# A kernel written out instruction by instruction, with a new order: two-block starts for the lone tiles, a weight piece loaded in two parts, three-block score runs from tile 8, one more store on GpSimd's queue

## The chip, the cores and the metric

The kernel runs on one core of a Trainium2 chip. The metric is the device time of one execution in microseconds (us). Three runs of the kernel before gave 213.09, 213.46 and 214.23 us, so the median is 213.46 us.

The engines are named as in the profile: PE is TensorE, with PEld for its weight loads; ACT is ScalarE, DVE is VectorE, POOL is GpSimd and SP is SyncE. Each works off its own instructions in order. Copies between device memory and on-chip memory are done by 16 DMA engines; an instruction on ACT, POOL or SP only issues them.

## The reference

Attention over 4 batches, 8 heads, 768 positions and 64 elements per head is followed by a two-layer network on the result. All inputs and the output are float32.

```
scores = scale * q @ k^T - slope[h] * distance       # each row sees 8 global positions and the last 96
a      = softmax(scores);   x = a @ v                 # x viewed as 3072 rows of 512
h = x @ w_in                                          # 512 -> 2048
out = (h - tanh(h)) @ w_out                           # 2048 -> 512
```

## The kernel before, in words

**Tiles.** The 3072 rows are 24 tiles of 128 rows. Tiles 0 to 3 are the first tiles of the four batches and see only themselves (one block of keys); tiles 4 to 23 see themselves (block 0) and the tile before in their batch (block 1). Because a row sees 96 positions back and 8 global ones, two blocks of 128 keys are enough: the 8 global keys and values are copied into the first rows of the back block (steps K and V).

**Steps of a tile u.** Each step has a name that the order list uses:

- `lq.u`, `lk.u`, `lv.u`: load q, k, v. The q and k of tiles 0 and 1 come as float32 over the queues of ACT and SP and are cast on chip (`cq`, `ck`); all else is cast on its way by POOL's queue.
- `T.u`: transpose k and q. For u below 7 PE does it (lines 309 to 322) and `Te.u.j` copies the result out of PSUM (a copy, lines 230 and 232); from tile 7 it is a DMA transpose on SP (line 334).
- `S.n`: one run of score matmuls (line 353), 8 per block. A run holds the blocks of one tile, or from tile THREES on three blocks of neighbouring tiles. `E.u.o` (ACT, line 360) is the exponential of a block, `M.u.o` (DVE, line 364) multiplies it by a mask that was made once (`bm`, PE line 276, and `em`, ACT line 281).
- `AV.u` (PE, line 379) is the product with v, `R.u` (DVE, lines 387 and 388) divides by the sums and writes x; `X.u` (PE, line 399) transposes x for tiles below 8 and `Xe.u` copies it out; from tile 8 on `Xe.u` is a DMA transpose on SP.
- `m1.g.f` (PE, line 421): first matmul for a group g of tiles and for some blocks f of 128 columns of w_in, accumulated in one PSUM bank. Groups 0 and 1 are the single tiles 0 and 1 (the lone tiles), groups 2 to 6 are pairs, groups 7 to 9 fours. A bank holds 512 columns, so a lone tile takes four blocks f at a time, a pair two and a four one. `th.g.f` (ACT, line 431) is the tanh, `g.g.f` (DVE, line 437) the difference; after it the bank is free.
- `m2.u.c.a` (PE, line 446): second matmul, four steps per tile; `ev.u` copies the bank out on ACT or DVE, `st.u` (line 455) stores it. The last tile, 23, is cut into columns 0 to 384 and 384 to 512.
- `in.j` and `out.j`: loads of w_in and w_out by POOL. The pieces of w_in end at the blocks listed in `in_end`. `zero:b` is a matmul on zeros into bank b (line 542) that computes nothing that is used.

**What sets the order.** Nothing is scheduled by a program at build time: the string ORDER (lines 17 to 66) lists every step once, and each engine gets its steps in the sequence of that list. The string HOMES (lines 67 to 105) says which buffer and which of the eight PSUM banks each result uses. A step waits for its inputs and for the last reader of its buffer or bank. POOL's list holds nearly all loads and all stores but the last ones, and a step there that waits holds up those behind it.

The lines that the change touches besides the two strings are 155 (THREES), 182 (in_end), 529 (blocks of an m1) and 539 (who stores).

Of the kernel before, what the change touches and what calls it, by code (L numbers as in the profile page):

```python
# [23 lines left out]
m1.2.2 g.1.4 th.2.6 T.4 g.2.6 th.2.2 lv.5 m1.2.0 Te.4.0/d Te.4.1/a lv.6 m1.1.8 g.2.2 th.2.0 g.2.0 m1.0.8 th.1.8 g.1.8  # L24
S.4 th.0.8 lq.6 m1.2.8 E.4.1 K.4 g.0.8 m1.1.12 th.2.8 M.4.1 T.5 E.4.0 g.2.8 m1.0.12 lk.6 Te.5.1/d Te.5.0/a m1.2.12
M.4.0 out.2 th.1.12 S.5 th.0.12 g.1.12 m2.1.0.0 th.2.12 K.5 g.0.12 E.5.0 m1.2.10 g.2.12 out.3 E.5.1 m2.0.0.0 M.5.0
lk.9 m2.0.0.1 th.2.10 M.5.1 lq.10 AV.4 g.2.10 lv.8 m2.2.0.0 V.4 R.4 AV.5 lk.7 m2.3.0.0 V.5 lq.8 R.5 m2.1.0.1 lk.10
m1.2.14 T.6 th.2.14 X.4 Te.6.1/d m2.2.0.1 Te.6.0/a lq.9 g.2.14 Xe.4/a m2.0.0.2 S.6 m2.2.0.2 E.6.0 K.6 lv.7 m2.1.0.2
E.6.1 M.6.0 X.5 m2.3.0.1 Xe.5/d M.6.1 m2.2.0.3 AV.6 T.7 ev.2.0/a m2.0.0.3 R.6 m2.3.0.2 T.8 ev.0.0/a V.6 m1.3.12 T.9
m1.3.0 th.3.12 T.10 m2.1.0.3 g.3.12 th.3.0 m1.3.8 g.3.0 ev.1.0/a S.7 st.1.0 th.3.8 lq.18 X.6 E.7.1 K.7 m2.3.0.3 g.3.8  # L30
lq.11 Xe.6/d m1.3.10 E.7.0 ev.3.0/d lv.12 m1.3.2 M.7.1 th.3.10 lq.14 m1.3.4 M.7.0 th.3.2 lv.10 g.3.10 S.8 th.3.4 g.3.2
m1.3.6 lq.12 E.8.1 g.3.4 m1.3.14 lv.9 th.3.6 M.8.1 AV.7 lk.13 E.8.0 g.3.6 m2.4.0.0 lk.11 R.7 th.3.14 m2.4.0.1 lk.12
V.7 S.9 M.8.0 lk.14 X.7 g.3.14 E.9.1 m2.4.0.2 st.0.0 K.9 Xe.7/d m2.4.0.3 E.9.0 lq.13 M.9.1 S.10 ev.4.0/d lv.11 AV.8
E.10.1 M.9.0 T.11 m1.4.8 K.10 R.8 E.10.0 m1.4.10 T.12 M.10.1 m2.5.0.0 th.4.8 M.10.0 Xe.8 th.4.10 AV.9 g.4.8 m1.4.2
T.14 V.9 m1.4.6 g.4.10 th.4.2 R.9 lq.23 T.13 AV.10 th.4.6 m1.4.0 g.4.2 lk.16 Xe.9 m2.5.0.1 g.4.6 th.4.0 R.10 m2.5.0.2
# [73 lines left out]
def kernel(  # L109
# [350 lines left out]
    def op(key, eng, fn):  # L460
        acts[".".join(map(str, key))] = (eng, fn)
# [128 lines left out]
```

## Time and profile before

| what | value |
|---|---|
| time of the profiled execution | 212.97 us |
| its span, first to last instruction | 211.1 us |
| the three timed runs | 213.09, 213.46, 214.23 us |
| PE busy | 203.6 us (96%) |
| DVE, ACT, POOL busy | 131.4, 118.8, 78.0 us |
| w_in pieces of 256 KB, 512 KB: median from issue to landing | 6.1 us, 10.7 us |
| stores by POOL: median from issue to landing | 3.2 us |

The profile is one execution. It lists the busy time of each engine, a picture of the span in 40 slices, the DMA queues, the chain of work that ended last (followed back from the last instruction), and groups of instructions by source line with their mean time and what ended the idle time before them. The trace behind it answers finer questions: busy time in a stretch of time, or the instructions of one engine in order. The time of the execution is 1.87 us longer than its span; that part lies around the first and last instruction.

### The profile page before, as it was taken

To read this page: it belongs to the slowest core of one execution; us is meant where nothing else is said; L and a number is where in the kernel's file an instruction comes from. 1 tells how busy PE (TensorE), PEld (TensorE's weight loads), DVE (VectorE), ACT (ScalarE), POOL (GpSimd) and SP (SyncE) were. 2 spreads that over 40 slices of the span, in tenths; PEclk is the share of its full clock that TensorE was granted. 3 is DMA by queue.
4 is the path that set the end of the run, shared out by engine and by line. 5 is a ranking of instruction groups with operands and counts; after the bars stand their busy time and mean duration, and the time that the engine had idled before them with its cause. 6 is when DMAs were issued, how large, how long until landed. Compare 5 with 4: busy or idle time off the path is not lost.

```text
span 211.1 us, 4634 instructions
## 1 busy us (share of the span) xinstructions
PE 203.6 (96%) x1854; PEld 122.4 (58%) x1879; DVE 131.4 (62%) x269; ACT 118.8 (56%) x175; POOL 78.0 (37%) x103
## 2 busy tenths in 40 slices
PE   8988999999999999999999999999999999999993
PEld 2558886557758765876665444555554444444442
DVE  7686787444898784789565779758875355412100
ACT  3995694245865385667645777268363364315322
POOL 8985546611992339259042360032000010003040
PEclk9999999999999999999999999999999999999999
DMA  6999999999999999999999979319311010003035
GB/s 154 208 191 195 198 192 163 197 156 197 158 153 170 170 156 177 146 166 172 215 132 145 152 121 182 66 59 101 76 28 26 0 50 0 3 0 149 0 135 213
DMA packets 100884, 27.29 MB, mean 129 GB/s; under 512 B 91840, under 2 KB 99264, under 8 KB 100864
## 3 DMA queue, kind: packets, MB, share of 16 engines
q0 software_dynamic: 72544, 18.62, 83.5%
q1 hardware_dynamic: 27776, 7.87, 23.5%
q10 hardware_dynamic: 544, 0.52, 0.9%
q8 instruction: 14, 0.23, 0.4%
q14 instruction: 6, 0.05, 0.1%
HBM read 27.26 MB, written 6.29 MB: 159 GB/s over the span
## 4 chain that ended last, share of the span: by engine, by line
PE 89%; DMA 4%; POOL 4%; issue 1%; ACT 0%; POOLq 0%
PE ps L446 39%; PE ps L421 39%; PE ps L353 5%; PE ps L379 5%; DMA w_in_bf<-in_moe_w_in_dram 4%; POOL vb L298 2%; POOL kq L295 1%; POOL w_in_bf L301 1%; PE ps L399 1%; PE ps L313 0%; PE ps L322 0%; POOL rel L236 0%; ACT ot L230 0%; POOLq L236 0%; POOLq L571 0%
## 5 line engine op out<-in xcount | busy, mean ns | idle before, releaser
L421 PE MATMUL ps<-xT,w_in_bf 128*128 128x256 bf16 (+2 forms) x635 | 90.9, 293 | 0.8 <-DMA w_in_bf<-in_moe_w_in_dram 0.6
L446 PE MATMUL ps<-w_out_bf,g 128*128 128x512 bf16 (+2 forms) x381 | 88.2, 370 | 1.4 <-issue 0.6
L437 DVE TENSOR_TENSOR g<-ps,th 128x512 bf16<-128x512 f32 x96 | 65.3, 687 | 37.8 <-ACT th L431 36.5
L431 ACT ACTIVATE th<-ps 128x512 f32<-128x512 f32 x96 | 57.2, 599 | 51.4 <-PE ps L421 48.3
L421 PEld LDWEIGHTS <-w_in_bf 128*128 128x128 bf16 x640 | 56.4, 98 | 29.0 <-DMA w_in_bf<-in_moe_w_in_dram 0.7
L446 PEld LDWEIGHTS <-g 128*128 128x128 bf16 x400 | 36.9, 98 | 38.1
L360 ACT ACTIVATE pr<-ps 128x1024 bf16<-128x1024 f32 x44 | 43.0, 1024 | 11.9 <-PE ps L353 11.9
L455 POOL DMA_DIRECT2D out_dram<-ot x21 | 12.1, 581 | 87.5 <-ACT ot L230 70.0
L364 DVE TENSOR_TENSOR pr<-pr,mk 128x1024 bf16<-128x1024 bf16 x44 | 29.3, 686 | 6.5 <-ACT pr L360 6.0
L298 POOL DMA_DIRECT2D kq<-in_q_dram x19 | 17.0, 902 | 22.0 <-DMA qk<-kq 17.6
L298 POOL DMA_DIRECT2D vb<-in_v_dram x24 | 21.7, 909 | 5.8 <-DMA w_in_bf<-in_moe_w_in_dram 4.0
L230 ACT COPY ot<-ps 128x512 f32<-128x512 f32 (+2 forms) x19 | 10.7, 563 | 21.9 <-PE ps L446 18.9
L298 POOL DMA_DIRECT2D kq<-in_k_dram x19 | 17.2, 919 | 8.5 <-DMA qk<-kq 6.5
L388 DVE TENSOR_TENSOR x<-ps,rden 128x512 bf16<-128x512 f32 x24 | 16.6, 691 | 0.8
L379 PEld LDWEIGHTS <-pr 128*128 128x128 bf16 x352 | 13.5, 97 | 4.2 <-DVE pr L364 0.6
L379 PE MATMUL ps<-vb,pr 128*128 128x65 bf16 x352 | 14.5, 193 | 0.2 <-DVE pr L364 0.2
L353 PEld LDWEIGHTS <-qk 64*128 64x128 bf16 x352 | 9.9, 94 | 6.1 <-issue 4.7
L353 PE MATMUL ps<-qk 64*128 64x128 bf16 x192 | 9.5, 218 | 0.1
L387 DVE RECIPROCAL rden<-ps 128x8 f32<-128x8 f32 x24 | 4.8, 200 | 4.8 <-PE ps L379 4.8
L353 PE MATMUL ps<-qk,qk 64*128 64x128 bf16 x160 | 7.8, 217 | 0.0
L542 PE MATMUL ps<-zero 128*128 128x512 bf16 x17 | 6.3, 489 | 1.0 <-DVE vb L272 1.0
L232 DVE COPY qk<-qk 128x32 bf16<-128x32 bf16 x16 | 3.3, 251 | 5.1 <-PE ps L353 5.1
(43 smaller groups left out, 60.6 us busy)
## 6 DMA issues: line engine op xcount, KB each, us to landing
out_dram<-ot POOLq DMA_DIRECT2D x21, 256.0 KB, 3.2
vb<-in_v_dram POOLq DMA_DIRECT2D x24, 128.0 KB, 5.6
kq<-in_k_dram POOLq DMA_DIRECT2D x22, 128.0 KB, 5.3
kq<-in_q_dram POOLq DMA_DIRECT2D x22, 128.0 KB, 5.4
w_out_bf<-in_moe_w_out_dram POOLq DMA_DIRECT2D x4, 512.0 KB, 11.5
w_in_bf<-in_moe_w_in_dram POOLq DMA_DIRECT2D x3, 512.0 KB, 10.7
f<-in_q_dram ACTq DMA_DIRECT2D x2, 256.0 KB, 4.3
f<-in_k_dram SPq DMA_DIRECT2D x2, 256.0 KB, 4.8
```

The source lines that it names most:

```text
L230: nc.scalar.copy(out=out, in_=in_)
L298: eng(e).dma_start(out=dst, in_=rows_of(src, u).rearrange("h p d -> p h d"))
L353: nc.tensor.matmul(bank(("s", u, o), hh)[:, p * P : (p + 1) * P], buf(("qk", back[u] if o else u))[r, 1, p, :], buf(("qk", u))[r, 0, p, :] ...
L360: nc.scalar.activation(d, banks(("s", u, o), 0, 1), AF.Exp, bias=0.0, scale=scale)
L364: nc.vector.tensor_tensor(out=t, in0=t, in1=mk[:, mask_of(u, o)], op=ALU.mult)
L379: nc.tensor.matmul(t[:, h // (H // 2), h % (H // 2), :], buf(("p", u, o))[:, slot(h), :], buf(("v", back[u] if o else u))[:, h, 0 : Dh + 1 ...
L388: nc.vector.tensor_tensor(out=buf(("x", u)).rearrange("q (a h) d -> q a h d", a=2), in0=t[:, :, :, 0:Dh], in1=rden.to_broadcast([P, 2, H / ...
L421: nc.tensor.matmul(t[:, (f - f0) * n : (f - f0 + 1) * n], w_in_bf[j][:, c, fo : fo + P], x[:, c, 0:n], start=(c == 0), stop=(c == CD - 1),)
L431: nc.scalar.activation(h_view(buf(("th", g, f0)), g, m), h_view(bank(("h", g, f0)), g, m), AF.Tanh, bias=0.0, scale=1.0)
L437: nc.vector.tensor_tensor(out=buf(("g", g))[:, f0 : f0 + m, 0:n], in0=h_view(bank(("h", g, f0)), g, m), in1=h_view(buf(("th", g, f0)), g, ...
L446: nc.tensor.matmul(bank(part)[:, 0 : c1 - c0], buf(("g", g))[:, f, t * P : (t + 1) * P], w_out_bf[f // FJ][:, f % FJ, c0:c1], start=(f == ...
L455: eng(e).dma_start(out=out[turn_of[u] * P : (turn_of[u] + 1) * P, c0:c1], in_=buf(("ot", u))[:, c0:c1])
```

## The change

Four lines of code change, and both strings are new:

- THREES goes from 11 to 8: tiles 8, 9 and 10, which had three runs of two blocks, now have two runs of three, so there are 19 runs of scores in place of 20, with later numbers one lower.
- `in_end` gets one more end: the 512 KB piece of w_in with blocks 4 to 7 is now two pieces of 256 KB, and there are six loads of w_in.
- The first four blocks of a lone tile are now two steps of two blocks, each with its own tanh and difference over 256 columns in place of one over 512.
- The store of tile 22 moves from SP's queue to POOL's.
- ORDER lists the steps in a new sequence on every engine, with 14 zero matmuls in place of 17; HOMES assigns buffers and banks anew. Some copies change engine with it. Counted by the two lists, ACT has seven steps more (a cast of k, a copy of a transposed tile, two copies of a transposed x, one copy-out of a result, two tanhs) and DVE three fewer.

```diff
 ORDER = """
-lq.1 lk.1 zero rel ones.0 zero:7 dist lk.3 lq.0 lk.0 zero:7 zero:7 slopes table lq.3 zero:7 zero:7 lk.2 turn first
-zero:7 ident bm.0 lq.2 ones.1 lv.0 bm.2 em.0 cq.1/d lv.1 zero:7 ck.1/d em.2 zero:7 T.1 lv.2 cq.0/a zero:7 ck.0/d in.0
-zero:7 Te.1.1/d Te.1.0/a zero:3 T.0 in.1 S.1 Te.0.1/d Te.0.0/a lv.3 T.3 E.1.0 S.0 Te.3.0/d zero:7 in.2 E.0.0 T.2 M.1.0
-lk.4 zero:6 zero:6 Te.2.1/d Te.2.0/a zero:6 lq.4 M.0.0 Te.3.1/a S.2 lk.5 E.2.0 AV.0 AV.1 R.0 S.3 in.3 E.3.0 R.1 X.0
-zero:1 lq.5 zero:3 Xe.0/a M.2.0 X.1 bm.1 Xe.1/a M.3.0 AV.2 in.4 em.1 m1.1.0 R.2 out.0 AV.3 th.1.0 X.2 R.3 m1.0.0
-Xe.2/a g.1.0 X.3 th.0.0 lv.4 m1.0.4 Xe.3/d g.0.0 m1.2.4 out.1 th.0.4 lq.7 m1.1.4 g.0.4 th.2.4 lk.8 g.2.4 m1.2.6 th.1.4
...
+lq.1 lk.1 zero rel ones.0 zero:7 slopes lk.2 lq.0 lk.0 zero:7 zero:7 table lq.2 dist zero:7 zero:7 lq.3 turn bm.1
+first lk.3 ident bm.0 ones.1 em.1 lv.1 cq.1/d zero:7 ck.1/a lv.0 zero:7 em.0 T.1 in.0 cq.0/a zero:7 ck.0/d lv.2 zero:7
+Te.1.0/d Te.1.1/a zero:3 T.0 lv.3 S.1 Te.0.1/d Te.0.0/a zero:6 zero:6 E.1.0 in.1 S.0 T.2 in.3 E.0.0 M.1.0 T.3 in.2
+Te.2.0/d zero:1 Te.2.1/a AV.1 M.0.0 Te.3.0/a lq.4 S.2 Te.3.1/a R.1 AV.0 lk.4 E.2.0 S.3 R.0 E.3.0 in.4 M.2.0 X.0 zero:3
+Xe.0/a in.5 M.3.0 AV.2 X.1 bm.2 R.2 Xe.1/a lk.5 AV.3 m1.0.0 em.2 R.3 m1.1.0 X.2 th.0.0 lq.5 X.3 th.1.0 Xe.2/d m1.1.2
+Xe.3/a g.1.0 m1.0.2 g.0.0 th.1.2 out.0 m1.2.2 th.0.2 g.1.2 g.0.2 m1.2.6 th.2.2 lv.4 g.2.2 m1.2.4 th.2.6 lk.6 g.2.6
...
-    THREES = 11
+    THREES = 8
...
-    in_end = [2, 4, 8, 12, 16]
+    in_end = [2, 4, 6, 8, 12, 16]
...
-        for f in range(0, CF, m):
+        for f, m in ([(0, 2), (2, 2)] if m == 4 else []) + [(f, m) for f in range(4 if m == 4 else 0, CF, m)]:
...
-            op(("st", u, c0), POOL if u < NU - 3 else SP, lambda e, u=u, c0=c0, c1=c1: store(e, u, c0, c1))
+            op(("st", u, c0), POOL if u < NU - 3 or u == NU - 2 else SP, lambda e, u=u, c0=c0, c1=c1: store(e, u, c0, c1))
```

Three more places of the new order, taken from it by engine. On SP the DMA transposes begin T.9 T.7 T.8 T.10 (before: T.7 T.8 T.9 T.10). On POOL the load of v for tile 8 stands behind st.1 and thirteen other loads: st.1.0 lv.7 lv.11 lq.14 lv.12 lv.16 lq.13 lq.11 lv.10 lv.9 lk.12 lq.12 lk.11 lk.14 lv.8. And the last stores on POOL are st.14 st.19 st.6 st.12 st.17 st.16 st.22 st.20 st.18, with the results of tiles 19, 17 and 20 in turn in output buffer 0, and those of tiles 22 and 21 in buffer 1.

More of the change, by code (lines that the diff above doesn't have):

```diff
@@ new lines @@
+th.2.10 m1.2.8 g.2.10 E.4.0 out.1 K.4 m1.1.8 E.4.1 M.4.0 out.2 m1.0.12 th.1.8 lq.9 M.4.1 th.2.8 T.5 g.1.8 th.0.12
+m1.1.12 Te.5.0/d Te.5.1/a g.0.12 m1.0.8 th.1.12 g.2.8 lv.5 m1.2.12 g.1.12 th.0.8 lq.10 g.0.8 m2.2.0.0 th.2.12 out.3
+g.2.12 m1.2.14 lk.7 m2.3.0.0 th.2.14 lk.9 g.2.14 T.6 AV.4 Te.6.1/d Te.6.0/a m2.0.0.0 V.4 R.4 m2.1.0.0 lq.7 S.5
+m2.2.0.1 E.5.1 K.5 m2.1.0.1 lk.8 E.5.0 M.5.1 m2.0.0.1 lq.8 M.5.0 S.6 lk.10 m2.1.0.2 E.6.1 K.6 m2.0.0.2 E.6.0 M.6.1
+AV.5 M.6.0 m2.3.0.1 R.5 X.4 m2.3.0.2 Xe.4/a V.5 X.5 m2.2.0.2 T.9 Xe.5/a AV.6 m1.3.0 T.7 R.6 m2.0.0.3 V.6 th.3.0 T.8
@@ new lines @@
+Xe.14 m2.9.0.2 V.14 g.6.6 AV.15 m2.9.0.3 R.15 m2.11.0.0 V.15 ev.9.0/a Xe.15 st.9.0 m2.11.0.1 lk.22 S.14 lv.20
+m2.10.0.0 E.17.0 K.17 st.7.0 m2.10.0.1 E.17.1 lv.18 M.17.0 m2.11.0.2 E.18.0 lq.22 M.17.1 AV.16 lv.22 m2.11.0.3 M.18.0
+R.16 lq.21 m1.7.7 ev.11.0/a V.16 Xe.16 lk.21 m2.10.0.2 th.7.7 st.8.0 g.7.7 m2.10.0.3 S.15 ev.10.0/a T.22 st.10.0
+m1.7.0 E.18.1 K.19 lq.20 m1.7.4 th.7.0 M.18.1 lk.23 E.19.0 m1.7.15 g.7.0 th.7.4 m1.7.13 M.19.0 th.7.15 g.7.4 T.21
+m1.7.10 th.7.13 g.7.15 m1.7.2 g.7.13 th.7.10 g.7.10 m1.7.1 th.7.2 g.7.2 AV.17 th.7.1 m1.7.3 V.17 E.19.1 g.7.1 T.20
@@ new lines @@
+m1.7.11 R.17 th.7.3 m1.7.6 g.7.3 T.23 th.7.11 M.19.1 m1.7.5 th.7.6 g.7.11 Xe.17 m1.7.12 g.7.6 th.7.5 g.7.5 AV.19
+th.7.12 m1.7.9 V.19 g.7.12 AV.18 R.19 th.7.9 m1.7.8 g.7.9 Xe.19 m1.7.14 th.7.8 R.18 m2.13.0.0 th.7.14 g.7.8 Xe.18
+g.7.14 m2.13.0.1 S.16 m2.13.0.2 E.20.1 K.20 K.21 m2.13.0.3 E.21.0 M.20.1 m2.12.0.0 ev.13.0/d E.20.0 M.21.0 m2.12.0.1
+M.20.0 S.17 m2.15.0.0 E.22.0 K.22 m2.15.0.1 E.21.1 M.22.0 AV.20 M.21.1 m2.15.0.2 E.22.1 R.20 m2.15.0.3 V.20 Xe.20
+M.22.1 S.18 ev.15.0/a AV.21 st.15.0 E.23.1 m1.8.1 R.21 st.13.0 E.23.0 st.11.0 m2.12.0.2 M.23.1 Xe.21 th.8.1 V.21
@@ new lines @@
+m1.8.4 M.23.0 g.8.1 AV.22 th.8.4 m1.8.9 V.22 R.22 m2.14.0.0 th.8.9 g.8.4 Xe.22 AV.23 g.8.9 m1.8.0 R.23 m1.8.15 th.8.0
+Xe.23 g.8.0 m1.8.8 th.8.15 g.8.15 m2.14.0.1 th.8.8 g.8.8 m1.8.3 m1.8.12 th.8.3 g.8.3 m1.8.5 th.8.12 g.8.12 m1.9.5
+th.8.5 g.8.5 m2.12.0.3 th.9.5 g.9.5 m1.9.9 ev.12.0/a m1.9.3 th.9.9 g.9.9 m1.9.1 th.9.3 g.9.3 m1.8.2 th.9.1 g.9.1
+m2.14.0.2 th.8.2 g.8.2 m1.8.7 m1.9.4 th.8.7 g.8.7 m1.8.14 th.9.4 g.9.4 m1.9.2 th.8.14 g.8.14 m1.8.6 th.9.2 g.9.2
+m1.9.6 th.8.6 g.8.6 m1.9.11 th.9.6 g.9.6 m1.9.14 th.9.11 g.9.11 m1.9.0 th.9.14 g.9.14 m2.18.0.0 th.9.0 g.9.0 m2.14.0.3
@@ new lines @@
+m2.16.0.0 ev.14.0/a st.14.0 m2.17.0.0 m2.22.0.0 m1.9.8 m2.16.0.1 th.9.8 g.9.8 m1.9.7 m1.9.15 th.9.7 g.9.7 m1.9.12
+th.9.15 g.9.15 m1.8.10 th.9.12 g.9.12 m1.8.11 th.8.10 g.8.10 m1.9.10 th.8.11 g.8.11 m2.22.0.1 th.9.10 g.9.10 m2.21.0.0
+m1.9.13 m2.18.0.1 th.9.13 g.9.13 m2.20.0.0 m2.20.0.1 m2.17.0.1 m2.19.0.0 m2.22.0.2 m1.8.13 m2.19.0.1 th.8.13 g.8.13
+m2.19.0.2 m2.17.0.2 m2.16.0.2 m2.16.0.3 m2.19.0.3 ev.16.0/a m2.18.0.2 ev.19.0/a st.19.0 m2.17.0.3 st.6.0 m2.21.0.1
+st.12.0 m2.22.0.3 ev.17.0/a m2.18.0.3 st.17.0 ev.22.0/a m2.20.0.2 st.16.0 st.22.0 ev.18.0/a m2.20.0.3 m2.21.0.2
@@ new lines @@
+kq.12:0 v.12:9 kq.13:1 v.13:5 kq.14:2 v.14:7 kq.15:3 v.15:6 kq.16:0 v.16:10 kq.17:1 v.17:4 kq.18:1 v.18:5 kq.19:3
+v.19:8 kq.20:2 v.20:0 kq.21:1 v.21:1 kq.22:0 v.22:9 kq.23:4 v.23:11 tr.0.0:5 tr.0.1:7 qk.0:1 s.0.0:2,3 p.0.0:1
+av.0:4,5 x.0:1 xt.0:0 xT.0:0 tr.1.0:6 tr.1.1:4 qk.1:0 s.1.0:0,1 p.1.0:0 av.1:0,1 x.1:0 xt.1:1 xT.1:1 tr.2.0:4 tr.2.1:5
+qk.2:2 s.2.0:2,3 p.2.0:2 av.2:2,3 x.2:2 xt.2:2 xT.2:2 tr.3.0:6 tr.3.1:7 qk.3:3 s.3.0:6,7 p.3.0:3 av.3:6,7 x.3:1 xt.3:3
+tr.4.0:3 tr.4.1:6 qk.4:4 s.4.0:0,1 s.4.1:6,7 p.4.0:4 p.4.1:0 av.4:4,5 x.4:0 xt.4:4 xT.3:3 tr.5.0:5 tr.5.1:0 qk.5:5
@@ new lines @@
+s.5.0:0,1 s.5.1:4,5 p.5.0:2 p.5.1:1 av.5:0,1 x.5:2 xt.5:5 tr.6.0:0 tr.6.1:6 qk.6:6 s.6.0:4,5 s.6.1:0,1 p.6.0:0 p.6.1:3
+av.6:0,1 x.6:1 xt.6:3 xT.4:1 qk.7:8 s.7.0:0,1 s.7.1:4,5 p.7.0:4 p.7.1:1 av.7:4,5 x.7:0 xt.7:3 qk.8:9 p.8.0:0 p.8.1:2
+av.8:6,7 x.8:0 xT.5:0 qk.9:7 s.8.0:0,1 s.8.1:4,5 s.9.0:6,7 p.9.0:3 p.9.1:1 av.9:6,7 x.9:2 qk.10:10 s.9.1:0,1
+s.10.0:4,5 s.10.1:6,7 p.10.0:1 p.10.1:4 av.10:2,3 x.10:1 xT.6:2 qk.11:5 p.11.0:3 p.11.1:0 av.11:4,5 x.11:2 qk.12:4
+s.11.0:6,7 s.11.1:4,5 s.12.0:2,3 p.12.0:2 p.12.1:4 av.12:2,3 x.12:0 xT.7:3 qk.13:1 s.12.1:2,3 s.13.0:4,5 s.13.1:0,1
@@ new lines @@
+s.22.0:4,5 s.22.1:0,1 p.22.0:0 p.22.1:2 av.22:4,5 x.22:1 qk.23:6 s.23.0:6,7 s.23.1:0,1 p.23.0:1 p.23.1:4 av.23:6,7
+x.23:2 h.0.0:0 th.0.0:0 g.0:1 h.0.2:5 th.0.2:3 h.0.4:2 th.0.4:1 h.0.8:2 th.0.8:3 h.0.12:4 th.0.12:0 h.1.0:1 th.1.0:1
+g.1:0 h.1.2:4 th.1.2:2 h.1.4:7 th.1.4:3 h.1.8:2 th.1.8:3 h.1.12:1 th.1.12:2 h.2.0:4 th.2.0:0 g.2:2 h.2.2:1 th.2.2:1
+h.2.4:6 th.2.4:2 h.2.6:0 th.2.6:0 h.2.8:3 th.2.8:1 h.2.10:5 th.2.10:2 h.2.12:0 th.2.12:0 h.2.14:1 th.2.14:1 h.3.0:4
+th.3.0:2 g.3:1 h.3.2:2 th.3.2:0 h.3.4:6 th.3.4:1 h.3.6:3 th.3.6:3 h.3.8:3 th.3.8:0 h.3.10:7 th.3.10:2 h.3.12:3
@@ new lines @@
+th.3.12:1 h.3.14:7 th.3.14:3 h.4.0:3 th.4.0:2 g.4:0 h.4.2:3 th.4.2:1 h.4.4:5 th.4.4:3 h.4.6:0 th.4.6:3 h.4.8:4
+th.4.8:2 h.4.10:0 th.4.10:0 h.4.12:0 th.4.12:1 h.4.14:2 th.4.14:0 h.5.0:5 th.5.0:1 g.5:2 h.5.2:0 th.5.2:1 h.5.4:1
+th.5.4:2 h.5.6:4 th.5.6:0 h.5.8:7 th.5.8:2 h.5.10:3 th.5.10:1 h.5.12:7 th.5.12:3 h.5.14:1 th.5.14:2 h.6.0:2 th.6.0:0
+g.6:1 h.6.2:7 th.6.2:2 h.6.4:6 th.6.4:3 h.6.6:6 th.6.6:1 h.6.8:0 th.6.8:3 h.6.10:6 th.6.10:0 h.6.12:5 th.6.12:0
+h.6.14:4 th.6.14:3 h.7.0:6 th.7.0:3 g.7:0 h.7.1:2 th.7.1:1 h.7.2:7 th.7.2:0 h.7.3:3 th.7.3:2 h.7.4:7 th.7.4:0 h.7.5:2
@@ L105 @@
+o.23.384:1
 """
```

113 lines of the change are left out of this document (34 added, 79 removed).

## The prediction

> **What bounds the kernel now.** I read the busy times first, then the busy time by stretch, then the chain that ended last, then PE's own rows at the start. The busy times:
>
> ```profile
> PE 203.6 (96%) x1854; PEld 122.4 (58%) x1879; DVE 131.4 (62%) x269; ACT 118.8 (56%) x175; POOL 78.0 (37%) x103
> ```
>
> PE is the bound, and no other engine is near it. By stretch (span and columns: stretch, its length, PE, PEld, DVE, ACT, POOL busy, granted clock, DMA share, GB/s):
>
> ```profile
> 0.00:18.43 18.43, 15.95 (x182) 8.94 (x184) 13.88 (x51) 13.37 (x18) 14.70 (x23) 1.00 1.34 186
> 18.43:60.00 41.57, 41.20 (x476) 30.41 (x482) 27.71 (x52) 25.89 (x39) 23.39 (x28) 1.00 1.74 180
> 60.00:120.00 60.00, 59.20 (x638) 40.22 (x646) 43.79 (x88) 36.68 (x51) 28.83 (x36) 1.00 1.63 164
> 120.00:165.00 45.00, 44.62 (x352) 22.68 (x358) 32.92 (x62) 25.92 (x39) 6.69 (x9) 1.00 0.57 80
> 165.00:207.84 42.84, 42.64 (x212) 20.13 (x212) 13.14 (x19) 16.72 (x30) 4.35 (x8) 1.00 0.16 58
> ```
>
> From 18.43 to 207.84 us PE idles 0.37 + 0.80 + 0.38 + 0.20 = 1.75 us of 189.4. Reordering has nothing to win there; it can only lose. What can shrink is the work in it, and the time before 18.43. The chain says what ends that time:
>
> ```profile
> 8.53 0.82 POOL vb L298
> 9.35 9.03 DMA w_in_bf<-in_moe_w_in_dram
> 18.38 0.05 issue
> 18.43 4.58 PE ps L421 x56
> ```
>
> The reader is to see that PE's dense part begins when the 512 KB piece of w_in (blocks 4 to 7, issued at 9.35) lands. PE's rows (start, length) just before it:
>
> ```profile
> 15.07 1.05 PE L421 MATMUL ps<-xT,w_in_bf 128*128 128x128 bf16 x16
> 15.96 0.41 PE L379 MATMUL ps<-vb,pr 128*128 128x65 bf16 x8
> 16.20 0.39 PE L399 MATMUL ps<-ident,x 128*128 128x128 bf16 x4
> 16.43 1.06 PE L421 MATMUL ps<-xT,w_in_bf 128*128 128x128 bf16 x16
> 17.46 0.40 PE L399 MATMUL ps<-ident,x 128*128 128x128 bf16 x4
> 18.43 4.58 PE L421 MATMUL ps<-xT,w_in_bf 128*128 128x128 bf16 x56 [0.57 <-DMA w_in_bf<-in_moe_w_in_dram]
> ```
>
> So at 18.43 PE has done T, S, AV and X of tiles 0 to 3, the three mask products, and m1 of both lone tiles for blocks 0 to 3. The question is when the new order has done the same list.
>
> **The start, step by step.** (1) Nothing moves up to S.1. T.0 waits for the cast of tile 0's k, which waits for a load that lands at 7.00 in both orders (DVE's cast there idles 1.48 us for it); S.1 stays at 8.08, E.1 and E.0 stay at 8.62 to 10.57. The cast of tile 1's k goes to ACT, between two mask exponentials: the first mask product ends at 4.0 (five warm-ups at 0.43 from 0.99, then two matmuls), the exponential starts 0.2 later, and 4.2 + 1.02 + 0.62 = 5.8, when T.1's weights were loaded before too (5.81), so nothing. (2) ACT now has three copies out of T.2 and T.3 in place of two, 0.55 each (row "1.10, x2"): E.2 starts at 10.45 + 3 x 0.55 = 12.1 (before 11.55), E.3 runs from 13.05 to 14.0 (before 12.74 to 13.76). This costs. (3) DVE gets that back. It does M.1, one copy and M.0 at a pace of 0.60 (starts 9.77, 10.37, 10.97), free at 11.6; before it then idled to 12.17 for an AV. Now AV.1 stands right behind M.1, so R.1 and R.0 (0.85 each) run from 11.6 to 13.35, M.2 to 14.0, M.3 after E.3 to 14.7; before M.3 ended at 15.14. (4) PE: X.0 at 13.45 (before 13.16), AV.2 at 14.05, X.1 and bm.2 (0.23 and 0.43), AV.3 at 15.05 (before 15.96). From there PE is dense: AV.3 0.3, m1.0.0 and m1.1.0 0.44 each (half of the 0.87 that 16 such matmuls take), X.2 and X.3 0.24 each, m1.1.2 and m1.0.2 0.44 each: 15.05 + 0.3 + 4 x 0.44 + 0.48 = 17.6. (5) m1.2.2 also needs the copy-out of X.3 on ACT. Before it stand em.2 (to 16.35) and two tanhs of 256 columns. No row shows that size: 128 columns take 0.265 (copy) and 512 take 0.60; I take 0.37, nearer the small end as in the 0.478 for 384. So Xe.3 runs from 17.05 to 17.6, and the list is done at 17.65: **0.78 us earlier**, by 0.57 of idle that goes and 0.2 of tighter packing.
>
> (6) Loads. The first 256 KB pieces take a median of 6.1 us from issue; the second, issued at 7.76, landed near 14.1, and 128 KB of v and 512 KB of w_in later it was 18.38: 6.7 ns per KB. In the new order blocks 2 and 3 lie behind one more v (15.0; needed 16.7), blocks 6 and 7 256 KB further (16.7; needed by m1.2.6 at 18.5), blocks 4 and 5 at the old end (18.4; needed by m1.2.4 at 19.4). What hides the split load is thus one step of m1 (m1.2.2) put ahead. If the piece were 1 us late, 0.1 would show. Two loads in place of one also cost POOL 0.78 us of issue, hidden since its loads then queue behind others for 9 us.
>
> Bounds of the start: a loss of 0.2 if the extra ACT copy (0.55) is not made good, and a gain of 1.1 if E.2's delay of 0.3 on M.3 does not count. I take 0.8.
>
> **Runs of three.** A run of 16 is followed by a hole or longer first matmuls:
>
> ```profile
> 41.95 0.55 PE ps L353 x16
> 42.50 0.16 issue
> ...
> 73.53 0.78 PE ps L353 x24
> ```
>
> Three runs of 16 become two of 24: 3 x 0.55 - 2 x 0.78 = 0.09, and one change-over less (0.10 to 0.16): **0.2 us**, bounds 0.1 and 0.3. The longer runs hold six banks of eight; after the second one, S.9, 2.8 us of other PE work precede AV.9, and the exponential and mask product that AV.9 waits for need 1.02 + 0.69 and some 0.3 of hand-overs, so that is covered by 0.8.
>
> **The rest at nothing.** ACT gets seven steps, some 3.5 us, against 92 us idle; DVE loses three. Three warm-up matmuls fewer leave holes that were filled with nothing. The end (last matmul at 207.84, span 211.10: 3.26) keeps its form: copy-out and store of the last 128 columns by SP. With tile 22's store on POOL, buffer 1 passes from 22 to 21 through POOL: ev.19, its store (2.8 to landing in the last rows), ev.17, ev.22, three stores of 0.55 of issue, 2.8 to landing, ev.21. Counted back from the last matmul, ev.19 ends 10.5 us before the end, ev.21 about 2.2 before it, and the last matmuls, which take its bank, start 0.9 before it: 1.3 us of room.
>
> **Sum.** 212.97 (profiled time) - 0.8 - 0.2 = 212.0. That execution is 0.49 under the median of 213.46; by that median it is 212.46. I predict **212.4**, nearer the median since timed runs carry no profiler. A measurement of this kernel can tell about 0.5% (1.07 us) from no change, so the border to faster is 212.39: the forecast lies on it.
>
> **The rivals.**
>
> *A, the start's gain is hidden (12%).* Xe.3, the m1.2.2 bank (freed by the difference for m1.1.0, at about 17.4) or a piece of w_in comes at 18.4 after all. For it: ACT carries E.2, E.3, two x copies, em.2, two tanhs and Xe.3 in one line. Against: each has 0.1 to 1 us to spare above. Time 212.4 + 0.8 = 213.2.
>
> *B, the array's pace falls back (10%), slower than before.* The row of granted clock says 1.00 throughout, but the first six warm-up matmuls stand 0.43 apart and three at 6.57 stand 0.215 apart: PE begins at half pace for 5 us of steady work. Before, PE was busy 0.71, 0.70 and 0.83 of each microsecond from 11 to 14 and kept the pace. In the new order, with fillers taken out, 10.75 to 13.45 holds only AV.0, S.2 and S.3: about 1.0 of 2.7. If that is under the point at which the pace falls, work from 14.05 on runs at half pace for 5 us and 2.2 us are lost: 212.4 + 2.2 = 214.6. Against: no single hole is above 1 us. The Trainium skill (TensorE: Matmul & The Clock Gate, Part 1: The HAM clock gate) states that the clock halves after an idle window of about 3.4 us; by that rule no hole here is long enough and B would not come.
>
> *C, a new wait in the dense part (8%).* First candidate is S.7 at about 51: SP sends T.9 before T.7, which costs 1.3 to 1.8 of issue, T.7 then leaves near 46.5 and lands 3.1 to 4.4 later, at 49.6 to 50.9. Second is AV.8 at 69: its v stands behind st.1 (about 50.3) and 13 loads of 0.9, issued at 62.6, landing 3.4 to 5.5 later. Third are banks: near the end a bank often returns after two m1 steps (1.73), and matmul to tanh to difference takes 1.52 (183.43 row group: difference ends at 185.81). Each could cost 0.3 to 1: 212.7 to 213.4.
>
> *D, more than the sum (8%).* Start 1.1 and runs 0.3, by the profiled time: 211.6.
>
> **How the numbers follow.** Forecast 62%, by itself 211.7 to 213.1; 37 points of it under 212.39. Faster: 37 + 8 (D) = 45%. Same: 25 + 12 (A) + 6 of C = 43%. Slower: 10 (B) + 2 of C = 12%. The range of 211.4 to 214.0 holds all but B and a few points at the ends.
>
> **What would show it.** Right: the dense part begins near 17.6 with no wait for w_in, the stretch from there to the last matmul is about 189.2 long, idle under 2 us in it, and the tail after it 3.3. Wrong: a wait for w_in or for Xe.3 before m1.2.2 (A); matmuls of 512 columns 0.43 apart after 14 us (B); PE waiting at S.7, AV.8 or in the last 45 us (C).

## The result, and the profile after

The kernel after takes 212.05 us (median of eight runs, 211.35 to 212.53); the kernel before, run beside it, takes 213.3 us (eight runs, 212.88 to 214.23). The ratio is 0.993, 95% interval 0.9911 to 0.9949: faster by 0.7%, and the interval lies just beyond the 0.5% that the forecast took as the least that can be told from no change. The forecast was 212.4. The profiled execution of after took 212.06 us with a span of 210.23; that of before 212.97 and 211.07 (the page rounds them to 210.2 and 211.1; the trace has the two decimals).

The busy times of after, and then its busy time by stretch (columns as before: stretch, its length, PE, PEld, DVE, ACT, POOL busy with counts, granted clock, DMA share, GB/s):

```profile
PE 202.4 (96%) x1851; PEld 122.3 (58%) x1876; DVE 130.0 (62%) x266; ACT 121.7 (58%) x182; POOL 79.2 (38%) x105
```

```profile
0.00:18.43 18.43, 14.82 (x181) 8.78 (x183) 12.49 (x49) 13.88 (x21) 15.29 (x24) 1.00 1.35 182
18.43:60.00 41.57, 41.30 (x481) 30.33 (x485) 27.51 (x52) 26.90 (x43) 22.96 (x28) 1.00 1.70 176
60.00:120.00 60.00, 59.42 (x635) 40.51 (x643) 43.52 (x85) 36.96 (x52) 32.54 (x41) 1.00 1.68 164
120.00:165.00 45.00, 44.62 (x352) 22.71 (x358) 34.21 (x64) 28.39 (x43) 3.57 (x6) 1.00 0.54 86
165.00:206.90 41.90, 41.74 (x204) 19.62 (x205) 12.30 (x18) 15.19 (x26) 4.82 (x9) 1.00 0.17 62
```

PE is the bound as before, idle for 0.27 + 0.58 + 0.38 + 0.16 = 1.39 us between 18.43 and 206.9 (1.75 before). The chain that ended last begins otherwise than before:

```profile
1.54 6.23 DMA f<-in_k_dram
7.77 0.02 issue
7.79 0.44 DVE kq L233
...
16.02 0.89 PE ps L422 x16
16.91 0.61 PE ps L400 x8
17.52 5.30 PE ps L422 x72
```

The 512 KB piece of w_in is gone from it. What ends last now is the load of tile 0's k, which lands at 7.79 in place of 7.00 and was not on the chain at all. PE's rows at the start say what it costs (start, length, operation, in brackets the idle time before it):

```profile
8.28 0.62 PE L319 MATMUL ps<-turn,kq 128*128 128x128 bf16 x8 [1.20 <-DVE kq L233]
...
14.10 0.40 PE L400 MATMUL ps<-ident,x 128*128 128x128 bf16 x4 [0.83 <-DVE x L389]
...
16.75 0.78 PE L400 MATMUL ps<-ident,x 128*128 128x128 bf16 x8
17.36 5.46 PE L422 MATMUL ps<-xT,w_in_bf 128*128 128x128 bf16 x72
22.75 0.64 PE L323 MATMUL ps<-turn,kq 128*64 128x128 bf16 x16
```

T.0 (the first row) waits 1.20 us for that k; from 14.10 PE runs on with no wait for w_in. The last row is T.4. Both orders have done the same work when T.4 begins, so its start is a mark that can be compared: 22.75 here, 22.94 before.

The other end of the span. The last copy-out of each kernel (ACT), before and after:

```profile
207.84 0.27 ACT L230 COPY ot<-ps 128x128 f32<-128x128 f32 x1 [0.41 <-PE ps L446]
```

```profile
207.44 0.27 ACT L231 COPY ot<-ps 128x128 f32<-128x128 f32 x1 [0.41 <-PE ps L447]
```

From its end to the end of the span, the tail, it is 211.07 - 208.11 = 2.96 us before and 210.23 - 207.71 = 2.53 us after (from the trace's times, which have a digit more). With T.4's start, the start of that copy-out and the two ends, each profile splits into three parts. The table has all profiles; "cast" is the cast of tile 0's k on DVE, whose start is the landing of that load (the cast itself takes 0.43 to 0.84 us, so T.4 is counted from its end):

| kernel | k of tile 0 lands | T.4 starts | T.4 less end of cast | T.4 to last copy-out | tail | span |
|---|---|---|---|---|---|---|
| before | 7.00 | 22.94 | 15.51 | 184.90 | 2.96 | 211.07 |
| after | 7.79 | 22.75 | 14.53 | 184.69 | 2.53 | 210.23 |
| again | 7.66 | 22.76 | 14.53 | 184.68 | 2.52 | 210.23 |
| a_sp22 | 7.28 | 22.34 | 14.63 | 184.69 | 2.96 | 210.25 |
| b_pool22 | 6.97 | 23.20 | 15.80 | 184.90 | 2.61 | 210.98 |
| a_pool21 | 7.43 | 22.78 | 14.54 | 184.68 | 2.57 | 210.30 |
| a_late0 | 8.89 | 24.92 | 15.60 | 184.68 | 2.99 | 212.85 |
| b_late0 | 9.05 | 25.73 | 15.84 | 184.90 | 2.89 | 213.78 |
| a_lone4 | 7.87 | 24.89 | 16.59 | 184.69 | 2.52 | 212.36 |
| a_lone4_x | 7.99 | 22.95 | 14.53 | 184.68 | 2.54 | 210.43 |
| a_piece | 8.37 | 24.18 | 15.38 | 184.96 | 2.53 | 211.94 |
| a_threes11 | 7.03 | 22.10 | 14.64 | 185.15 | 2.51 | 210.03 |
| a_loads | 7.79 | 22.76 | 14.54 | 184.69 | 2.53 | 210.23 |
| b_loads | 7.40 | 23.26 | 15.21 | 184.92 | 2.94 | 211.38 |

So the 0.83 us between the two spans are 22.94 - 22.75 = **0.19 from the start**, 184.90 - 184.69 = **0.21 from the dense part** and 2.96 - 2.53 = **0.43 from the end**. The forecast had 0.8, 0.2 and nothing. The sum was met by other terms than those that were added up, and the experiments ask why.

Each profile is one execution, and the split is that of this pair. The medians differ by more, 1.25 us. Three of after's eight runs have a span of 209.5 in place of 210.2 to 210.7. With the dense part and the tail of the profile, T.4 begins at about 22.0 in them (an estimate), 0.9 before T.4 of before. In those runs the start would give its 0.8, if it is the part that is shorter in them; no profile of them shows it.

### The profile page after: what moved, and what is told of

The parts are those of the page before. It is cut to its first block, busy times and chain, and to the rows that moved or that the text cites. A ratio compares the mean times of both kernels' runs of the same rounds, so it can differ in the third digit from the quotient of the medians.

```text
span 210.2 us, 4631 instructions
## 1 busy us (share of the span) xinstructions
PE 202.4 (96%) x1851; PEld 122.3 (58%) x1876; DVE 130.0 (62%) x266; ACT 121.7 (58%) x182; POOL 79.2 (38%) x105
## 4 chain that ended last, share of the span: by engine, by line
PE 92%; DMA 3%; DVE 2%; issue 1%; ACT 1%; SPq 0%
PE ps L422 40%; PE ps L447 39%; PE ps L354 5%; PE ps L380 5%; DMA f<-in_k_dram 3%; PE ps L400 1%; DVE pr L365 1%; DVE x L389 1%; ACT pr L361 0%; PE ps L314 0%; SPq L296 0%; PE ps L319 0%; DVE qk L233 0%; ACT qk L231 0%; PE ps L323 0%
## 5 line engine op out<-in xcount | busy, mean ns | idle before, releaser
L422 PE MATMUL ps<-xT,w_in_bf 128*128 128x256 bf16 (+2 forms) x634 | 89.6, 293 | 0.3
L438 DVE TENSOR_TENSOR g<-ps,th 128x512 bf16<-128x512 f32 (+1 forms) x98 | 65.5, 676 | 31.8 <-ACT th L432 30.8
L432 ACT ACTIVATE th<-ps 128x512 f32<-128x512 f32 (+1 forms) x98 | 57.3, 590 | 45.5 <-PE ps L422 40.5
L231 ACT COPY ot<-ps 128x512 f32<-128x512 f32 (+2 forms) x20 | 11.3, 564 | 21.0 <-PE ps L447 15.8
L543 PE MATMUL ps<-zero 128*128 128x512 bf16 x14 | 5.3, 483 | 1.0 <-DVE zero L464 1.0
```

The costliest lines, as they stand in the source:

```text
L231: nc.scalar.copy(out=out, in_=in_)
L422: nc.tensor.matmul(t[:, (f - f0) * n : (f - f0 + 1) * n], w_in_bf[j][:, c, fo : fo + P], x[:, c, 0:n], start=(c == 0), stop=(c == CD - 1),)
L432: nc.scalar.activation(h_view(buf(("th", g, f0)), g, m), h_view(bank(("h", g, f0)), g, m), AF.Tanh, bias=0.0, scale=1.0)
L438: nc.vector.tensor_tensor(out=buf(("g", g))[:, f0 : f0 + m, 0:n], in0=h_view(bank(("h", g, f0)), g, m), in1=h_view(buf(("th", g, f0)), g, ...
```

## The experiments

Names that begin with a_ are the kernel after with one edit, those with b_ the kernel before with one. Times are medians; each ratio is to the kernel before, run beside it, with its 95% interval. Single runs of one kernel spread by over 1 us, so an effect under about half a us is read from the profiles, in the table above, and not from the times.

### The kernel after once more

again: no edit.

> The kernel after, unchanged, once more. It shows what of its one profile is chance. Theory (the start hangs on one load): the time from the landing of tile 0's k (end of the wait of the cast on VectorE, 7.77 us in the first profile) to the first m1 step of the pair (18.40) is again 10.6 us, whatever the landing is; with a landing at 7.0 as in the profile before, the dense part starts at 17.6 and the span is 209.5, with 7.8 it is 210.2. Rival (the new order itself makes that load late): the landing is again 7.7 to 7.8. The end after the last copy-out was 2.49 us against 2.99 before; if it hangs on the order, it is 2.5 again. Time against before: ratio 0.993, some 1.0 to 1.5 us less.

212.06 us, ratio 0.9941 (0.9915 to 0.9967). All three parts of its profile are within 0.01 us of those of after, the landing within 0.13. In this pair the parts are steady enough to be compared by tenths; the start is not so in all executions, since the ten spans of this run go from 209.4 to 210.9.

### The stores at the end

a_sp22 gives tile 22's store back to SP, b_pool22 makes the same edit in before, a_pool21 moves one store more:

```diff
 # a_sp22, in after
-POOL if u < NU - 3 or u == NU - 2 else SP
+POOL if u < NU - 3 else SP
 # b_pool22, in before
-POOL if u < NU - 3 else SP
+POOL if u < NU - 3 or u == NU - 2 else SP
 # a_pool21, in after
-POOL if u < NU - 3 or u == NU - 2 else SP
+POOL if u < NU - 1 else SP
```

> After, with the store of tile 22 back on SyncE's queue; nothing else. Theory (the moved store shortens the end): the time from the end of the last copy-out to the end of the span goes from 2.5 back to 3.0 us, and the kernel is 0.4 to 0.5 us slower than after. Rival (my prediction: the store costs nothing where it is, the shorter end is chance): 0.0 us, end anywhere from 2.5 to 3.0.

> Before, with the store of tile 22 on GpSimd's queue; nothing else. Theory of the end: the time after the last copy-out goes from 2.99 to 2.5 us, ratio to before 0.998. Rival: 1.000. Beside it, its start is that of before: the dense part starts at 18.4 (when the 512 KB piece lands) even if tile 0's k lands later than 7.0, up to 7.6.

> After, with the store of tile 21 on GpSimd's queue too, so that SyncE stores only the two parts of the last tile. Theory of the end, taken further: each store less on SyncE's queue gives up to 0.4 us, so 0.2 to 0.4 us faster than after. Rival: no change, since that store is issued over 2 us before the last one.

a_sp22: 211.9 us, ratio 0.9934 (0.9904 to 0.9965), tail 2.96. b_pool22: 212.84 us, ratio 0.9988 (0.996 to 1.0016), tail 2.61. a_pool21: 212.2 us, ratio 0.9943 (0.9922 to 0.9965), tail 2.57. So the edit makes the tail 0.43 us shorter in after and 0.35 in before, and a second store moved gains nothing more: a gain per store fell. The times alone can't show 0.4 us here (a_sp22 is not above again).

What SP waits for in its last instructions (columns: in total, times, longest), in before, in after and in a_pool21:

```profile
SPq L585 <- DMA out_dram<-ot: 1.2, 1, 1.2
```

```profile
SPq L586 <- DMA out_dram<-ot: 0.7, 2, 0.4
```

```profile
SPq L586 <- DMA out_dram<-ot: 0.8, 2, 0.5
```

Before, SP waits once, for the very last store, and what follows that wait still takes time. After, it waits for an earlier store first and for the last store at the end. The trace names the semaphore that each DMA of SP signals at its end, and those that SP's last instructions wait for. SP's DMAs, with ACT's two loads counted among them, take eight semaphores in turn, and the closing waits go through the eight in the order in which they were first taken. Before issues 39 DMAs from SP, 41 with ACT's, and its last store falls on the first of the eight (41 is 5 x 8 + 1). The wait for it ends at 209.72, and seven waits for transfers that ended long ago still follow, 0.06 us apart, the last at 210.15. After issues 38, and its last store falls on the last semaphore: the wait for it, over at 209.32, is the last of the eight. a_pool21 issues 37: one wait follows. The last store lands 1.60 us behind the last copy-out in before and in after, so the store itself is not what got shorter.

### One load more on SP

These two put another load of 256 KB, into a buffer that nothing reads, ahead of tile 0's k on SP's queue. They were meant for the start (how far does each kernel hang on that load?), but they also bring the count of SP's DMAs to 39 in after and 40 in before, with all stores where they were.

```diff
+    extra = pool.tile([P, H * Dh], FP32, name="extra")
+    op(("xk",), SP, lambda e: load_rows(e, extra.rearrange("q (b f) -> q b f", b=2), k, 2))
 # ORDER
-lk.0
+xk lk.0
```

> After, with one more 256 KB float32 load (rows of tile 2 into a buffer that nothing reads) on SyncE's queue ahead of the load of tile 0's k. It makes that k land later by 1 to 1.5 us. Theory (after hangs on that load one for one): the dense part starts 10.6 us after the landing, and the time grows by the whole delay, 1.0 to 1.5 us. Rival (the start of after hangs on the w_in pieces or on the queues of ScalarE and VectorE from constants on): 0 to 0.5 us.

> Before, with the same extra load. Theory: before has about 0.57 us of slack between the end of its start chain (17.86 with the landing at 7.0) and the landing of the 512 KB piece of w_in (18.38), so that it loses 0.4 to 0.6 us less than after does from the same delay, if the piece does not land later itself (256 KB more on the DMA engines may make it 0.5 to 1 later, which would take the slack away: then the loss is the same as in after, and the wait for w_in is still in the profile). Rival: the same loss and no wait for w_in.

a_late0: 215.23 us, ratio 1.0081 (1.0044 to 1.0118). b_late0: 215.58 us, ratio 1.0099 (1.0063 to 1.0135).

By the medians the load costs after 3.2 us and before 2.3, more than was expected of either.

The end: a_late0 has tile 22's store on POOL, as after has, and yet a tail of 2.99; its SP waits as before's does, once:

```profile
SPq L588 <- DMA out_dram<-ot: 1.2, 1, 1.2
```

b_late0, with 40 DMAs, has six waits after its last store and a tail of 2.89. So it is the count of SP's DMAs that sets the tail, not whose queue stores tile 22. With 38 it is 2.51 to 2.61 (eight profiles), with 37 2.57, with 40 2.89, with 39 2.94 to 2.99 (four): about 2.53 plus 0.06 us for each wait that follows the last store. (The 2.61 is b_pool22, whose last store landed 1.70 us behind the copy-out; in nearly all others it is 1.6.)

The start: the load was 1.10 us later in a_late0 than in after, and T.4 began 2.17 us later. The other 1.07 is pace. PE's row for T.0 in a_late0, and its busy time by stretch (stretch, length, PE busy, granted clock, DMA share, GB/s):

```profile
9.38 1.03 PE L319 MATMUL ps<-turn,kq 128*128 128x128 bf16 x8 [2.29 <-DVE kq L233]
```

```profile
8.00:10.00 2.00, 0.62 (x7) 0.75 1.67 189
10.00:12.00 2.00, 2.00 (x18) 0.50 2.03 173
12.00:14.00 2.00, 2.00 (x49) 0.89 2.17 164
```

After a hole of 2.29 us the granted clock is 0.50, and 18 matmuls fill 2 us. b_late0 has a hole of 2.15 and 0.57 and 0.58 in the stretches from 10 to 14. So neither profile is a clean measure of how much of a late load each kernel hides. The one run of each whose mean granted clock is 1.00 has a span of 212.0 (a_late0) and 212.7 (b_late0), 1.8 and 1.6 over the profiles of after and before, or 1.3 and 1.7 without the change of the tail. That gives no sign that before hides more, but where the load landed in these two runs is not known.

When the clock falls can be read more closely. The trace's record of it goes by periods of 3.41 us. In a_late0, b_late0 and a_piece (below) it is 0.50 for one such period, and PE was busy for 1.49, 1.26 and 1.64 us of the period before. In the other profiles with such a record no period ahead of T.4, counted from the one at which the record begins, with 1.00, has less than 1.90 us (a_pool21), and none is followed by a fall. The two periods of a_piece, and the lowest ones of a_pool21 and of after (columns as above):

```profile
7.09:10.50 3.41, 1.64 (x26) 1.00 1.88 173
10.50:13.91 3.41, 3.41 (x57) 0.50 1.95 175
```

```profile
4.82:8.23 3.41, 1.90 (x14) 1.00 1.34 229
```

```profile
5.18:8.59 3.41, 2.02 (x19) 1.00 1.36 214
```

So what goes with a fall in these profiles is a period of which PE was busy for less than about half, not the length of one hole; and a period can begin anywhere against the kernel (at 5.18 in after, at 7.09 in a_piece). After had little to spare.

### Lone tiles in one step of four blocks

a_lone4 undoes the two-block steps and leaves the order; a_lone4_x also moves tile 1's step behind X.3, its tanh and difference accordingly, and its bank:

```diff
-for f, m in ([(0, 2), (2, 2)] if m == 4 else []) + [(f, m) for f in range(4 if m == 4 else 0, CF, m)]:
+for f in range(0, CF, m):
 # ORDER of both: without m1, th and g of .0.2 and .1.2
 # ORDER of a_lone4_x besides
-R.3 m1.1.0 X.2 th.0.0 lq.5 X.3 th.1.0 Xe.2/d Xe.3/a g.1.0 g.0.0 out.0 m1.2.2
+R.3 X.2 th.0.0 lq.5 X.3 Xe.2/d m1.1.0 Xe.3/a g.0.0 th.1.0 out.0 m1.2.2 g.1.0
 # HOMES of a_lone4_x
-h.1.0:1
+h.1.0:4
```

> After, with the first four blocks of a lone tile as one step again (m1.0.0 and m1.1.0 of 16 matmuls at the places of the first halves). Theory (the second halves are what PE does while x of tiles 2 and 3 is copied out): X.2 and X.3 come 0.87 us later, the copy-out of X.3 ends some 0.9 to 1.3 us after X.3, and PE waits 0.7 to 1.1 us before m1.2.2; 0.6 to 1.0 us slower than after. Rival (only the DMA landing counts): within 0.2 us of after.

> As the run before it, but with X.2 and X.3 between the two steps of 16 matmuls and m1.1.0 in another bank, so that the second step covers the copy-out. Theory (cover is what counts, not the size of the step): within 0.2 us of after. Rival (two-block steps themselves are needed, by their shorter tanh before the copy-out on ScalarE): 0.4 to 0.8 us slower than after, with a wait before m1.2.2.

a_lone4: 213.24 us, ratio 0.9989 (0.9957 to 1.0022): by the median all of the gain is lost. But its ten runs spread: four have spans of 210.5 to 210.7, near after's, and six of 211.2 to 212.4; the profile is of the longest. Its rows on PE name two waits:

```profile
17.46 1.51 PE L422 MATMUL ps<-xT,w_in_bf 128*128 128x128 bf16 x24 [0.91 <-DMA w_in_bf<-in_moe_w_in_dram]
...
20.39 4.58 PE L422 MATMUL ps<-xT,w_in_bf 128*128 128x256 bf16 x56 [0.97 <-DVE g L438]
```

Tile 0's step now wants blocks 2 and 3 before X.2 and X.3, at about 16.5, and they land at 17.41; and m1.2.2 waits 0.97 for its bank, which the longer tanh and difference of tile 1 give back later. The expectation had a wait of that size there, for the copy-out of X.3.

a_lone4_x: 212.14 us, ratio 0.9939 (0.9922 to 0.9957); T.4 stands 14.53 behind the cast, as in after, with the same large steps. Its tile 0 too wants blocks 2 and 3 at about 16.5, but here the trace has them at 15.85, and PE does not wait. So the first of a_lone4's waits came of a late landing (the nine other profiles with that piece have it at 15.53 to 16.90), and the second of the order and the bank, which a_lone4_x mends with the step as large as before. With a k that lands at 7.99 the gain thus does not need the smaller step or the shorter tanh. Whether it does when the k lands early is not shown: the seven spans of a_lone4_x are all 210.2 to 210.5, while after has 209.5 in three of eight.

### The third piece of w_in in one load

```diff
-in_end = [2, 4, 6, 8, 12, 16]
+in_end = [2, 4, 8, 12, 16]
 # ORDER: in.2 left out, in.3 in.4 in.5 become in.2 in.3 in.4
```

> After, with blocks 4 to 7 of w_in as one load of 512 KB again, at the place of the first of the two pieces. My prediction's sum: that load lands near 18.4 to 18.9 by its place in the queue, m1.2.6 wants it at 18.5 to 19.3: a wait of 0 to 0.4 us and a time within 0.2 us of after. Rival (the split is what removed the wait for w_in): the wait of 0.5 us or more is back before m1.2.6, 0.5 us slower.

212.56 us, ratio 0.9949 (0.9924 to 0.9974): within the noise of after. The profile is of the longest of its five runs: the k of tile 0 landed at 8.37, the hole before T.0 was 1.93, and the granted clock fell to 0.63 (10 to 12 us) and 0.52 (12 to 14), so that work came later than in after and the piece was there in time. What it does show is when the load of 512 KB landed, at 18.77. In after m1.2.6 begins at 19.27 (m1.2.2 at 18.40 and 0.87 for it), so a landing like this one would have been in time by 0.5. With the k at 7.03, as in a_threes11, m1.2.6 would begin at 18.6 and wait 0.2 (both are estimates). And two of the five runs have a span of 209.6, where after's shortest is 209.5. A wait of 0.5 in every run, as the rival has it, does not fit that. One landing is too little to say that the split is worth nothing. One wait of 0.2 in the dense part, for a transposed q and k, is new there (184.96).

### Runs of two for tiles 8 to 10

```diff
-    THREES = 8
+    THREES = 11
 # ORDER: S.9 and later one number up; a new "S.9 K.9" ahead of E.9.0
```

> After, with three runs of two blocks for tiles 8 to 10 in place of two runs of three (S.9 set before E.9.0, the rest of the order kept). The sum's term: PE's dense part, from m1.2.2 to the last matmul (189.0 us in after's profile), is 0.2 us longer, bounds 0.1 and 0.3. Rival (the change-over between runs costs nothing): 0.09 us; rival (a new wait at the added run, since its banks come free only shortly before): 0.5 us or more with PE idle near 60 us.

212.2 us, ratio 0.9955 (0.9925 to 0.9985). The dense part is 185.15, that is 0.46 longer than in after, beyond the bounds of 0.1 and 0.3. All of it lies between the first of the three runs, S.8, and the X behind the last. PE's rows for the first run of three in after, and then for the last run of two in a_threes11:

```profile
56.74 0.40 PE L354 MATMUL ps<-qk 64*128 64x128 bf16 x8
56.97 0.39 PE L354 MATMUL ps<-qk,qk 64*128 64x128 bf16 x8
57.20 0.39 PE L354 MATMUL ps<-qk 64*128 64x128 bf16 x8
57.51 1.05 PE L422 MATMUL ps<-xT,w_in_bf 128*128 128x256 bf16 x8
```

```profile
61.66 0.40 PE L354 MATMUL ps<-qk 64*128 64x128 bf16 x8
61.89 0.39 PE L354 MATMUL ps<-qk,qk 64*128 64x128 bf16 x8
62.40 0.38 PE L400 MATMUL ps<-ident,x 128*128 128x128 bf16 x4
```

24 score matmuls take 57.51 - 56.74 = 0.77 with the change-over behind them; 16 take 62.40 - 61.66 = 0.74 here, and 0.60 and 0.56 in the other two runs: 1.90 for three runs against 2 x 0.77 = 1.54, and the run that is more has 0.09 of change-over ahead of it too. From there on the two profiles run in parallel. Before's own three runs of two take 0.55 each by the same measure (56.28 to 56.83, 60.90 to 61.45, 63.51 to 64.06), 1.65 in all: a_threes11's cost 0.25 more.

This kernel also had the earliest k of all with after's start, at 7.03, and the earliest T.4, at 22.10.

### The sequence of POOL's first loads

a_loads gives after the sequence lk.3 lq.3 lk.2 lq.2 lv.0 lv.1 lv.2 in.0 that before has, b_loads gives before lk.2 lq.2 lq.3 lk.3 lv.1 lv.0 in.0 lv.2:

```diff
 # a_loads: POOL's first eight loads
-lk.2 lq.2 lq.3 lk.3 lv.1 lv.0 in.0 lv.2
+lk.3 lq.3 lk.2 lq.2 lv.0 lv.1 lv.2 in.0
 # b_loads: the reverse
```

> After, with GpSimd's first eight loads in the sequence of before (tile 3's k and q, tile 2's k and q, v of tiles 0, 1 and 2, then the first piece of w_in); nothing else. In eight profiles with the start of after, tile 0's k (a float32 load on SyncE's queue that shares the DMA engines with these loads) landed at 7.0 to 8.4 us, median 7.7; in the two with the start of before, at 7.0 and 7.0. Theory (the sequence of GpSimd's first loads makes it late): it lands at 7.0 here, the first X of tile 2 follows its cast's end by 8.53 us as in every profile of after, and the median is 0.4 to 0.7 us under after's 212.05. Rival (the landing is chance, or comes from something else in the start): landing anywhere from 7.0 to 8.4 and a median within 0.2 us of after.

> Before, with GpSimd's first eight loads in the sequence of after. Theory: tile 0's k lands later, at 7.3 to 8.4; up to some 0.6 us of that is hidden behind the landing of the 512 KB piece of w_in at 18.4 to 18.7, which stays, so the median is 0 to 0.4 us over before's 213.3. Rival (chance): landing at 7.0 and the time of before within 0.1 us.

a_loads: 212.06 us, ratio 0.9941 (0.9917 to 0.9964); k of tile 0 lands at 7.79, as in after. b_loads: 213.74 us, ratio 1.0011 (0.9986 to 1.0036); it lands at 7.40, later than in before but inside the spread of the others. My theory that this sequence makes the load late in after fell: giving the sequence back does not bring 7.00 back in the profile, and the median is that of after. Whether the sequence does something in before (7.40 against 7.00 and 6.97) is not shown by one profile.

## Why the prediction was right, and where it was not

**The time and the sign** held: 212.05 against 212.4, inside the range, on the faster side of the border that the forecast lay on. By the profiled time the sum was 1.0, measured 0.91. In that pair of profiles two of its three terms were wrong and their errors cancelled, so that the number fits so well is in part luck.

**The start, step (1) failed.** "Nothing moves up to S.1", since the load of tile 0's k "lands at 7.00 in both orders". It landed at 7.79 in after, and in nine profiles with after's start and no load added anywhere from 7.03 to 8.37; with before's, at 7.00 and 6.97, and at 7.40 with the loads of b_loads. SP issues it at 1.54 in both. Why it lands later is open: in after the sequence of POOL's first loads is not it.

**Steps (2) to (5) held from the cast on.** The walk had 10.65 us from the landing to m1.2.2; measured 18.40 - 7.79 = 10.61 (X.3 ends at 17.52, and two m1 of 0.44 each stand ahead of m1.2.2). Where after's k did land at 7.03 (a_threes11), T.4 began at 22.10, which is 0.84 before T.4 of before with its 7.00: the 0.78 of the sum. The wait for w_in is gone, and its cover with it: before hides a part of a late k in that wait (b_loads: the cast ends 0.62 later, T.4 starts 0.32 later and the wait is gone), after passes each tenth on (T.4 stands 14.53 to 14.64 behind the end of the cast in seven profiles), and more where the clock falls (a_piece, 8.37). Before hangs on the 512 KB piece instead: in b_pool22 the piece lands at 18.65 in place of 18.38, and T.4 starts at 23.20 in place of 22.94 although the k is early.

**Step (6)** held, with both sides of it 0.6 to 1.0 us too early. The sum had the three pieces at 15.0, 16.7 and 18.4; the trace of after has them at 15.74, 17.69 and 18.95. They are asked for at 17.52, 19.27 and 20.14, where the sum had 16.7, 18.5 and 19.4. The room was 1.8, 1.6 and 1.2 us against 1.7, 1.8 and 1.0. It is not always so much: with an earlier k and a later piece (7.28 and 16.90 in a_sp22, 7.03 and 16.65 in a_threes11) m1.1.2 would ask at about 17.1 and 16.9, which leaves 0.2 us (an estimate from T.4, 5.23 us behind in after). The two loads in place of one show no wait in after; what one load would have cost is not settled, though by a_piece's one landing, 18.77, it would be 0 to 0.2. The tanh of 256 columns takes 0.393 (estimate 0.37).

**Runs of three:** 0.2 forecast, and the two kernels' dense parts differ by 0.21. Undone in after the runs are worth 0.46. The rest, 0.25, is what a_threes11 (185.15) has over before (184.90), and it is also what its three runs of two cost over before's, 1.90 against 1.65. Three quarters of that lie in the last run (0.74 against 0.55). No wait in the profile names the cause, and it stays open.

**The end: the term that was costed at nothing and was 0.43.** The forecast said that the end "keeps its form: copy-out and store of the last 128 columns by SP". The store is the same. What changed is how many of SP's closing waits come after it, because one DMA less on SP shifts the turn of the eight semaphores. The room on bank and buffer, which the step worked out at length, was enough: no wait shows there.

**The rivals.** A (the gain hidden) came for most of the start's gain in the profiled execution (0.19 of 0.78 is left), by a door that was not listed: not w_in or Xe.3, but the first load. B (the pace falls back) did not come in the thin stretch from 10.75 to 13.45, where the granted clock stayed at 1.00 in after (PE was busy for 2.36 us of the period from 12.01 to 15.42). The stretch was also less thin than the forecast counted: 2.18 us of work, or 1.52 if it is moved by the 0.79 that the k came later, in place of 1.0. Its mechanism exists, a little earlier in the kernel: holes of 1.93, 2.15 and 2.29 us before T.0 (a_piece, b_late0, a_late0) came with 3.41 us at 0.50, holes of 1.20 (after) and 1.39 (a_lone4_x) did not. The Trainium skill (TensorE: Matmul & The Clock Gate, Part 1: The HAM clock gate) states an idle window of about 3.4 us, free-running. The periods of 3.41 us, which begin at another time in each profile, agree with a window of that size; that the window has to be idle does not, since PE was busy for up to 1.64 us of those that were followed by a fall, and the measurement decides. C came nowhere in after: PE's waits from 22 to 208 us are one of 0.2 us for an issue, none at S.7, at AV.8 or near the end.

## What to carry to other kernels

When a wait is taken off the chain of waits, ask what it was covering: the release next in time takes its place, and here it was a load whose landing differs by over a microsecond between nine kernels with the same sequence of DMAs on SP. Holes at the start cost twice once PE is busy for less than about half of one of the clock's periods, so a filler matmul in front of an uncertain load may be worth its place; no run here tried one. And when one profile explains a loss, see whether the other runs had it: two of the profiles above were of the longest run of their kernel. When a change moves a DMA from one queue to another, look at the end of the span too: a count that decides which of the closing waits comes last can be worth as much as the edit itself.

## What the runs showed of the hardware that I had not expected

- The closing waits on SP stand 0.06 us apart, and those that follow the last store are paid in full: tails from 2.51 to 2.99 us, by the count of DMAs on that queue, and in one profile (b_pool22) by 0.1 us more through a later landing of the last store.
- The same load of 256 KB, issued at 1.54 us, landed 5.5 to 6.8 us later in nine kernels that have the same sequence on SP; a piece of w_in of the same size, issued at 8.8 to 9.3 us, took 6.7 to 8.6 in ten.
- The granted clock fell to half for 3.41 us after a period of 3.41 us in which PE was busy for 1.26 to 1.64 us, and stayed after periods with 1.90 or more. It need not fall at the hole: in a_piece the hole ended at 8.86 and the clock fell at 10.50, and the first matmuls after the hole still ran at full pace.
